# One core, attention and a top-1 mixture of experts: new planner numbers, one last store behind all branches

## The chip, the core and the metric

The kernel runs on one core of one Trainium2 chip. The metric is the device time of one execution in microseconds (us). Five engines work side by side, each with its own list of instructions: TensorE (PE, matrix products and transposes), VectorE (DVE), ScalarE (ACT), GpSimd (POOL) and SyncE (SP), which here issues most of the transfers. An engine runs its list in the order in which it was written; an instruction whose input is not there holds up everything behind it on that engine.

## What is computed

The input is q, k, v of shape (4, 8, 576, 64) and a small memory per head. Attention comes first, and its rows are the tokens of the second part:

```python
scores = scale * np.matmul(q, k.transpose(0, 1, 3, 2))
scores = np.where(causal, -1000000000.0, scores)
scores = scores - scores.max(-1, keepdims=True)
a = np.exp(scores)
a /= a.sum(-1, keepdims=True) + 1e-09
local = np.matmul(a, v)
...
return (g * mem_out + (1 - g) * local).astype(np.float32)
```

Here mem_out is phi(q) times the memory matrix of the head over phi(q) times its norm vector. Then 2304 tokens of 512 numbers are each sent to one of 8 experts:

```python
expert_idx = np.argmax(logits, axis=1)
...
gate_w = probs[np.arange(N), expert_idx]
for e in range(E):
    mask = expert_idx == e
    h = np.maximum(x[mask] @ w1[e], 0.0)
    out[mask] = gate_w[mask, None] * (h @ w2[e])
```

with w1 of 512 x 1024 and w2 of 1024 x 512 per expert.

## The kernel before

**Attention** is cut into 8 groups (a batch, four heads), each with five blocks of query rows, 112 units in all. A unit is worked on by four engines in turn: scores on PE (S, lines 685 and 693), mask and row minimum on DVE (M, line 696), the exponential on ACT (E, lines 724 and 726), transposes of the result on PE (T, lines 733 and 737), copies of the transposed blocks out of the matrix engine's memory on ACT (line 745) or DVE (line 747), and the product with v on PE (C, lines 760 and 768). When the units of a block are done, the assembly adds the memory's share: its matrix product on PE (line 846), a copy on ACT (line 861), small quotients on DVE (lines 867, 887, 897), a product on DVE (Xl, line 907), another on POOL (A, line 913) and their sum on POOL (line 919). The routing then reads the finished rows (line 955 on ACT squares and sums them, lines 969 to 976 cut them in two halves of 16 bits).

**What sets the order.** The class Sched (lines 40 to 185) is a planner. Each operation has an engine, or a list of engines to choose from, a duration, what it depends on, buffers and a priority. The planner simulates the engines and writes the instructions out in the order in which its simulation starts them. The durations of ACT and DVE come from c_act and c_dve (lines 23 and 27), the time after which another engine may use a result from LAT (line 44), that for the same engine from line 109, and the priorities from the table PRIO (line 37), an entry of which ('ra', 'rr', 'aA' and others) can also say which engines an operation may go to. Where the plan leaves PE idle, line 270 puts small filler products. The first steps of the expert part, three tiles of tokens among them, are planned by the same class: the weights come by DMA as 32-bit numbers and are split into a leading part (line 1292 on ACT, 1304 for the second matrix) and a rest (line 1294 on DVE), and the tokens of a tile are gathered by POOL (line 1436).

**The expert loop** is written by hand, one slot of 128 tokens after another: gather the tokens by their row numbers (ix, loaded by SP at line 1421; gather at line 1436 on POOL), transpose and split them, first product (line 1499), relu (line 1508), transposes (line 1512), split (lines 1516 and 1520), second product (line 1526), times the gate value (y_out, line 1532 on DVE, into one of three buffers ys), and a store to the rows of the output that ix names (y_store, an indirect DMA on POOL, line 1550). Slots 0 to 14 (NFIX = 15) always run. Slots 15 to 24 are nested branches: whether a slot has tokens is read from a table (line 1669), and its instructions run only if it has (when, lines 1747 and 1751). With these inputs 19 slots and three tiles ahead of them run, 22 stores in all. The result of slot i-1 is multiplied in slot i's code, and stored in the branch of slot i or, if that is not taken, in its Else arm, the last store of the run.

Of the kernel before, what the change touches and what calls it, by code (L numbers as in the profile page):

```python
# [20 lines left out]


def c_act(n, ptr=False):
    return (284 if ptr else 170) + 0.84 * n


def c_dve(n):
    return 150 + 1.042 * n


def c_pool(n):
# [2 lines left out]

BG = 200.0

PRIO = {'po': {'S': -5.883137309853216, 'M': -5.687372506837317, 'E': 1.1512438895455412, 'T': -2.3534222843976242, 'H': -2.2397011500929547, 'L': -4.132349736948786, 'C': -0.056339306635263986}, 'pa': 1.8585493879096298, 'pv': -5.3741376405058645, 'sq': -21.965205397914144, 'xt': 2, 'ra': 0, 'aD': 1, 'ps': 1.7384297857956093, 'lv': 25.117654926616954, 'pr': 0.9204950267468823, 'rs': 0, 'w1p': 182.12895601615688, 'ag': 0, 'pb': 8.752629265291922, 'lqk': -7.732031619747982, 'rr': 2, 'aA': 1, 'pe4': 2, 'ep': 144.67457595060114, 'w2p': 291.50948210051763, 'slack': 37.2962196981224, 'pp': 1.1250262799121031, 'fc': (1, 2), 'nw2l': 3, 'nw1l': 4, 'xlo': 1, 'wpd': 1, 'w1': 300000, 'ND': 2, 'avl': 2, 'ph': 3, 'avc': 1, 'phat': -15373.102132059515, 'ae': 1, 'rp': 2, 'vhe': 1}


class Sched:  # L40


    TWO = {"xh", "xl", "w1l", "w2l", "exl", "A", "ad", "b", "p", "cu", "est", "eor", "tab", "gn", "gl", "gr"}
    LAT = dict(PE=250, ACT=200, DVE=200, POOL=200, SP=0, NOP=0)

    warm_from, warm_to, warm_ns, warm = 0.0, 0.0, 110, None

# [14 lines left out]
    def run(self, slack=80.0):  # L62
# [15 lines left out]
        while ready:  # L78
            cand = {}
            for o in ready:  # L80
                ts = o["at"]
                ok = True
                for m, al in enumerate(o["alloc"]):
                    ring = al[0]
                    if len(al) > 3:
                        if holder[ring][al[3]] is not None:
                            ok = False
                            break
                        ts = max(ts, self.rings[ring][al[3]])
                        continue  # L90
                    res = (al[2] if len(al) > 2 else 0) + sum(x[0] == ring for x in o["alloc"][:m])
                    fr = sorted(t for t, h in zip(self.rings[ring], holder[ring]) if h is None)
                    if len(fr) <= res:
                        ok = False
                        break
                    ts = max(ts, fr[res])
                if not ok:
                    continue
                best = None
                for eng, dur, fn in o["alts"]:  # L100
                    t = max(ts, free_at.get(eng, 0.0))
                    if eng in port and shares(o, eng):
                        t = max(t, port["DVE" if eng == "POOL" else "POOL"])
                    for d in o["deps"]:
                        p = self.byname[d]
                        if p["xfer"] is not None:
                            lat = 200
                        elif p["eng"] == eng:
                            lat = 0 if eng in ("PE", "SP", "NOP") else (100 if eng == "POOL" else 125 if eng == "DVE" else 120)
                        else:  # L110
                            lat = self.LAT[p["eng"]]
                        t = max(t, p["end"] + lat)
                    if best is None or t + dur < best[1] + best[2]:
                        best = (eng, t, dur, fn)
                cand.setdefault(best[0], []).append((best[1], o["prio"], o["n"], o, best))
# [60 lines left out]
def kernel(  # L176
# [14 lines left out]
    nc = tc.nc  # L191
# [1336 lines left out]
            )  # L1528

    def y_out(i):  # L1530
        ys = big("ys")[(i + NEARLY) % 3]
        nc.vector.tensor_scalar(ys, G[i]["yp"], G[i]["gg"], None, op0=ALU.mult)  # L1532
        G[i]["ys"] = ys

# [9 lines left out]

    out_w = []

    def y_store(i):
        if i < 0:
            nc.gpsimd.memset(pause, 0.0)
        ins = nc.gpsimd.indirect_dma_start(  # L1550
            out=out[:, :], out_offset=bass.IndirectOffsetOnAxis(ap=G[i]["ix"][:, 0:1].bitcast(U32), axis=0),
            in_=G[i]["ys"], in_offset=None, bounds_check=NTOK - 1, oob_is_err=False,
        ).ins

        if i < 0:
            for o in out_w:
                tc.declare_no_dep(ins, o, reason="rows of the output")
            out_w.append(ins)
# [175 lines left out]
    def second(i):  # L1734
        w_dma(2, regs[i]["nx"], cond=regs[i]["pf"])
        if i + 1 < NSLOT:
            gather_g(i + 1)

    def rest(i):

        if i == NSLOT:
            l2(i - 1)
            y_store(i - 1)
            return
        ch_reg(i)
        pf_regs(i)
        with when(i, CALC):  # L1747
            first(i, False)
        l2(i - 1, i)

        with when(i, ALL) as go:
            y_store(i - 1)
            fetch(i + 4)
            second(i)
            rest(i + 1)
        with go.Else():
            y_store(i - 1)

    ch_reg(0)
    pf_regs(0)  # L1760
# [5 lines left out]
    for i in range(NFIX):  # L1766
        first(i)
        l2(i - 1, i)
        y_store(i - 1)
        second(i)  # L1770
    rest(NFIX)


_INS = ["q", "k", "v", "M_prev", "z_prev", "beta", "moe_expert_emb", "moe_tau", "moe_w1", "moe_w2"]
# [26 lines left out]
```

## Time and profile before

| | us |
|---|---|
| median of 3 runs | 542.04 |
| lowest and highest of them | 541.66 and 547.07 |
| the profiled execution, own time | 542.65 |
| its span in the profile | 540.9 |
| PE busy | 515.7 (95%) |
| DVE, ACT, POOL busy | 322.0, 308.8, 185.8 |

The span runs from the first to the last instruction; the own time holds some 1.8 us around it. A share of busy time is an average over parts of the kernel with different limits, so the rows below take it apart by stretches: the attention part up to about 230 us, the passage to the experts up to about 300, the expert loop up to 524, and the end. In a timeline row the bracket says how long the engine had been idle before this instruction and whose result ended the wait.

### The profile page before, as it was taken

To read this page: it belongs to the slowest core of one execution; us is meant where nothing else is said; L and a number is where in the kernel's file an instruction comes from. 1 tells how busy PE (TensorE), PEld (TensorE's weight loads), DVE (VectorE), ACT (ScalarE), POOL (GpSimd) and SP (SyncE) were. 2 spreads that over 40 slices of the span, in tenths; PEclk is the share of its full clock that TensorE was granted. 3 is DMA by queue.
4 is the path that set the end of the run, shared out by engine and by line. 5 is a ranking of instruction groups with operands and counts; after the bars stand their busy time and mean duration, and the time that the engine had idled before them with its cause. 6 is when DMAs were issued, how large, how long until landed. Compare 5 with 4: busy or idle time off the path is not lost. (4 is left out here: it accounts for less than half of the span.)

```text
span 540.9 us, 11357 instructions
## 1 busy us (share of the span) xinstructions
PE 515.7 (95%) x3506; PEld 440.8 (81%) x3506; DVE 322.0 (60%) x1024; ACT 308.8 (57%) x608; POOL 185.8 (34%) x259
## 2 busy tenths in 40 slices
PE   7999999999999999998999999999999999999970
PEld 5888988898898988887877888888888888888850
DVE  5776877777886877777972142522366516863360
ACT  5887877677886877596622252422365526744340
POOL 6101424434443433338445332122331222212221
PEclk9999999999999999999999999999999999999995
DMA  7658745235542311376409846732379846884221
GB/s 156 152 65 186 166 98 118 44 77 133 127 104 46 79 41 41 78 255 154 100 12 243 262 108 217 176 80 59 75 237 320 226 97 213 237 229 152 60 61 34
DMA packets 127471, 71.93 MB, mean 133 GB/s; under 512 B 111385, under 2 KB 111513, under 8 KB 127395
## 3 DMA queue, kind: packets, MB, share of 16 engines
q1 hardware_dynamic: 122242, 59.49, 43.4%
q0 software_dynamic: 5152, 11.57, 7.4%
q8 instruction: 30, 0.49, 0.4%
q14 instruction: 47, 0.38, 0.4%
HBM read 111.74 MB, written 10.67 MB: 226 GB/s over the span
## 5 line engine op out<-in xcount | busy, mean ns | idle before, releaser
L1526 PE MATMUL L<-RC,hhl 128*128 128x512 f32 x528 | 129.0, 394 | 0.3 <-PEq L1747 0.3
L1499 PE MATMUL aux<-RB 128*128 128x512 f32 x528 | 125.8, 392 | 1.6 <-ACTq L1451 1.1
L1499 PEld LDWEIGHTS aux<-RB 128*128 128x128 f32 x528 | 98.3, 188 | 22.6 <-ACTq L1451 1.2
L1526 PEld LDWEIGHTS L<-RC,hhl 128*128 128x128 f32 x528 | 97.5, 188 | 19.9 <-issue 0.7
L1520 DVE TENSOR_TENSOR hhl<-aux,hhl 128x512 fp32r<-128x512 f32 x46 | 31.5, 689 | 118.3 <-ACT hhl L1516 61.4
L760 PE MATMUL L<-VN,aT 128*128 128x128 f32 x640 | 87.3, 276 | 0.0
L760 PEld LDWEIGHTS L<-VN,aT 128*128 128x128 f32 x640 | 79.0, 192 | 2.0 <-DVE aT L747 1.1
L1516 ACT ACTIVATE hhl<-aux 128x512 fp32r<-128x512 f32 x46 | 27.2, 595 | 77.2 <-PE aux L1512 43.1
L696 DVE CUSTOM_DVE_ANT_0 a<-aux,mask 128x128 f32<-128x128 f32 (+3 forms) x144 | 62.2, 451 | 13.7 <-PE aux L685 9.9
L724 ACT ACTIVATE a<-a,nb 128x128 f32<-128x128 f32 (+3 forms) x128 | 65.2, 557 | 0.8 <-DVE nb L696 0.5
L1550 POOL DMA_INDIRECT out_dram<-ys,ix x22 | 22.6, 1026 | 123.5 <-DVE ys L1532 116.3
L733 PE MATMUL aux<-ident,a 128*128 128x128 f32 x384 | 62.4, 280 | 2.6 <-ACT a L724 2.6
L745 ACT ACTIVATE aT<-aux 128x512 f32<-128x512 f32 (+3 forms) x89 | 44.5, 512 | 30.0 <-PE aux L733 29.2
L913 POOL TENSOR_TENSOR A<-ms,dd 128x256 f32<-128x256 f32 x32 | 21.7, 677 | 92.4 <-DVE dd L897 47.9
L733 PEld LDWEIGHTS aux<-ident,a 128*128 128x128 f32 x384 | 43.0, 141 | 12.4 <-ACT a L724 4.4
L1508 ACT ACTIVATE hs<-aux 128x512 f32<-128x512 f32 x44 | 23.9, 595 | 46.6 <-PE aux L1499 46.1
L1436 POOL DMA_INDIRECT a<-x_dram,ix x26 | 28.0, 1075 | 48.3 <-DMA ix<-id_dram 16.5
L1387 DVE TENSOR_TENSOR RB<-RA,RB 128x1024 fp32r<-128x1024 f32 x24 | 29.2, 1225 | 9.1 <-ACT RB L1383 7.8
L1387 DVE TENSOR_TENSOR RC<-RA,RC 128x1024 fp32r<-128x1024 f32 x24 | 27.9, 1221 | 1.7 <-ACT RC L1383 1.5
L1383 ACT ACTIVATE RB<-RA 128x1024 fp32r<-128x1024 f32 x24 | 25.2, 1059 | 6.2 <-PE aux L1499 5.6
L1443 POOL DMA_INDIRECT gg<-gate_dram,ix x23 | 24.6, 1067 | 7.8 <-issue 6.1
L846 PE MATMUL aux<-Mb,qp 128*128 128x130 f32 (+1 forms) x160 | 25.3, 281 | 0.5 <-ACT a L724 0.5
(255 smaller groups left out, 766.1 us busy)
## 6 DMA issues: line engine op xcount, KB each, us to landing
RA<-in_moe_w_dram SPq DMA_DIRECT2D x78, 1024.0 KB
RA<-in_moe_w_dram SPq DMA_DIRECT2D x16, 512.0 KB
RA<-in_k_dram SPq DMA_DIRECT2D x32, 128.0 KB
RA<-in_q_dram SPq DMA_DIRECT2D x32, 128.0 KB
VN<-in_v_dram SPq DMA_DIRECT2D x32, 128.0 KB
x_dram<-x SPq DMA_DIRECT2D x16, 256.0 KB
RA<-in_k_dram SPq DMA_DIRECT2D x8, 64.0 KB
RA<-in_q_dram SPq DMA_DIRECT2D x8, 64.0 KB
```

Source lines behind the costliest of these rows:

```text
L696: nc.vector.tensor_tensor_reduce(out=o, in0=i0, in1=i1, op0=ALU.add, op1=ALU.min, scale=-0.125, scalar=init, accum_out=acc)
L724: nc.scalar.activation(out=a[:, c], in_=a[:, c], func=AF.Exp, scale=-1.0, bias=nb[:, y : y + 1])
L733: nc.tensor.transpose(ps[:, P * y : P * y + P], a[:, P * y : P * y + P], ident)
L745: nc.scalar.activation(out=u["aT"][0:r, o : o + n], in_=t[0:r, 0:n], func=AF.Copy)
L760: nc.tensor.matmul(lt[:, P * hh : P * hh + P], u["aT"][:, P * y : P * y + P], vt[:, c : c + P], start=kb == 0, stop=kb == i)
L846: nc.tensor.matmul(m[rr, 130 * x : 130 * x + 130], qp[:, x, P * i : P * i + n], Mb[b % 2][:, 2 * g + x, :], start=True, stop=True,)
L1387: nc.vector.tensor_tensor(l, s, h.bitcast(F32), op=ALU.subtract)
L1436: nc.gpsimd.indirect_dma_start(out=xg, out_offset=None, in_=x_dram[0:rows, :], in_offset=bass.IndirectOffsetOnAxis(ap=ix[:, 0:1].bitcast(U ...
L1499: nc.tensor.matmul(G[i]["hp"][n], a[:, cc], w[:, c, 512 * n : 512 * n + 512], start=c == 0 and a is xh and w is w1h, stop=c == KD - 1 and ...
L1516: nc.scalar.activation(out=big("hhl")[n][:, 0:512], in_=G[i]["gps", n], func=AF.Copy)
L1520: nc.vector.tensor_tensor(t[:, 512:1024], G[i]["gps", n], t[:, 0:512].bitcast(F32), op=ALU.subtract)
L1526: nc.tensor.matmul(G[i]["yp"], t[:, cc : cc + P], w[:, c, :], start=c == 0 and a == 0 and w is w2h, stop=c == KF - 1 and a == 1)
```

## The change

First, the planner's numbers. The fixed part of an ACT operation falls from 170 (284 with a pointer operand) to 112 (225), that of a DVE operation from 150 to 85; the time until another engine may read the result rises from 200 to 260 and 270, and for the same engine from 120 and 125 to 170 and 180. The priorities are set anew, and with 'aA' the product A may also go to DVE. The matrix products stay the same, but 39 fillers stand where 46 stood, 11 of 32 products A go to DVE, and ten copies of transposed blocks go from DVE to ACT.

Second, the last store. The Else arms with their store go. In each branch taken, and once ahead of the first, POOL copies the row numbers of the slot to a tile of its own (keep, into lix). From slot 14 on all results use one buffer of ys, and one store behind all branches writes that buffer to the rows in lix.

```diff
 def c_act(n, ptr=False):
-    return (284 if ptr else 170) + 0.84 * n
+    return (225 if ptr else 112) + 0.84 * n
...
 def c_dve(n):
-    return 150 + 1.042 * n
+    return 85 + 1.042 * n
...
-    LAT = dict(PE=250, ACT=200, DVE=200, POOL=200, SP=0, NOP=0)
+    LAT = dict(PE=250, ACT=260, DVE=270, POOL=200, SP=0, NOP=0)
...
-                            lat = 0 if eng in ("PE", "SP", "NOP") else (100 if eng == "POOL" else 125 if eng == "DVE" else 120)
+                            lat = 0 if eng in ("PE", "SP", "NOP") else (100 if eng == "POOL" else 180 if eng == "DVE" else 170)
...
     def y_out(i):
-        ys = big("ys")[(i + NEARLY) % 3]
+
+        ys = big("ys")[(i + NEARLY) % 3 if i < NFIX - 1 else 0]
...
-    def y_store(i):
+    def y_store(i, ix=None):
         if i < 0:
             nc.gpsimd.memset(pause, 0.0)
+        ix = G[i]["ix"] if ix is None else ix
         ins = nc.gpsimd.indirect_dma_start(
-            out=out[:, :], out_offset=bass.IndirectOffsetOnAxis(ap=G[i]["ix"][:, 0:1].bitcast(U32), axis=0),
+            out=out[:, :], out_offset=bass.IndirectOffsetOnAxis(ap=ix[:, 0:1].bitcast(U32), axis=0),
...
+    lix = cst.tile([P, 2], I32, name="lix")
+
+    def keep(i):
+        nc.gpsimd.tensor_copy(lix, G[i]["ix"])
+
     def rest(i):
 
         if i == NSLOT:
             l2(i - 1)
-            y_store(i - 1)
             return
...
-        with when(i, ALL) as go:
+        with when(i, ALL):
             y_store(i - 1)
+            keep(i)
             fetch(i + 4)
             second(i)
             rest(i + 1)
-        with go.Else():
-            y_store(i - 1)
...
+    keep(NFIX - 1)
     rest(NFIX)
+    y_store(NFIX - 1, lix)
```

The order of instructions, at three places. The first is PE, group 7 of 8, from a pair of units' scores (128x384, the first two of six rows stand) to the transposes of its first unit, which take the exponentials a_3344 before and a_3341 now. Before:

```order
L685 MATMUL aux_3323<-RB_81 128x384
L685 MATMUL aux_3324<-RB_81 128x384
...
L733 MATMUL aux_3334<-ident_71,a_3248 128x128 x2
L846 MATMUL aux_3341<-Mb0_89,qp1_85 64x130 x2
L768 MATMUL L_3309<-VN2_88,aT_3288 128x130 x5
L733 MATMUL aux_3364<-ident_71,a_3279 128x128 x4
L760 MATMUL L_3373<-VN0_86,aT_3318 128x128 x2
...
L733 MATMUL aux_3400<-ident_71,a_3300 128x128 x4
L846 MATMUL aux_3408<-Mb1_90,qp0_84 128x130 x2
L760 MATMUL L_3373<-VN0_86,aT_3353 128x128 x2
L627 MATMUL aux_3423<-ident_71,RA_80 128x128 x4
L733 MATMUL aux_3431<-ident_71,a_3344 128x128 x3
```

and now:

```order
L685 MATMUL aux_3307<-RB_81 128x384
L685 MATMUL aux_3308<-RB_81 128x384
...
L760 MATMUL L_3128<-VN2_88,aT_3179 128x128 x4
L768 MATMUL L_3335<-VN2_88,aT_3195 128x130 x5
L846 MATMUL aux_3351<-Mb0_89,qp1_85 64x130 x2
L733 MATMUL aux_3357<-ident_71,a_3286 128x128 x4
L733 MATMUL aux_3364<-ident_71,a_3341 128x128 x3
```

Of the work that stood between, eight narrow products of the routing (at the second mark), the scores of another pair, and several blocks have gone elsewhere.

The second place is ACT at the first conversion of weights to the experts' form (L1292, which waits for a DMA). The rows L724 are exponentials, L745 copies, L861 those of the assembly. Before:

```order
L724 ACTIVATE a_3803<-a_3803,nb_3804 128x256 x2
L745 ACTIVATE aT_3858<-aux_3848 128x256
L861 ACTIVATE ms_3879<-aux_3852 64x260
L1292 ACTIVATE RB_81<-RA_80 128x1024
L745 ACTIVATE aT_3941<-aux_3914 128x512
L724 ACTIVATE a_3899<-a_3899,nb_3900 128x384
L745 ACTIVATE aT_3960<-aux_3946 128x512
L861 ACTIVATE ms_3970<-aux_3955 128x260
L724 ACTIVATE a_3928<-a_3928,nb_3929 128x384
```

and now:

```order
L724 ACTIVATE a_3818<-a_3818,nb_3819 128x256 x2
L745 ACTIVATE aT_3924<-aux_3905 128x512
L724 ACTIVATE a_3911<-a_3911,nb_3912 128x384
L1292 ACTIVATE RB_81<-RA_80 128x1024
L724 ACTIVATE a_3927<-a_3927,nb_3928 128x384
L745 ACTIVATE aT_3960<-aux_3930 128x512
L861 ACTIVATE ms_3970<-aux_3954 128x260
L724 ACTIVATE a_3945<-a_3945,nb_3946 128x384
L745 ACTIVATE aT_3992<-aux_3948 128x384
```

One more exponential (a_3911, of 384 columns) stands ahead of the first conversion, and the one of its pair directly behind it.

The third place is the end of POOL's list. Before, each Else arm is like the one whose rows stand here (a semaphore update, shown as ISA, the store, another update, a jump, and then the next arm):

```order
L1796 ISA
L1550 DMA out_0_dram<-ys_4575,ix_3902 2304x512
L1751 ISA
L1751 UNCONDITIONAL_BRANCH
L1796 ISA
```

and now the arms hold an update and a jump, and behind the last of them stand the store and the end:

```order
L1757 ISA
L1757 UNCONDITIONAL_BRANCH
L1552 DMA out_0_dram<-ys_4561,lix_4805 2304x512
L1803 UNCONDITIONAL_BRANCH
L1803 ISA
```

The store has moved from the arm to a place behind the jump, and the arm's update from behind the store to ahead of it.

## Rows read from the trace of the kernel before

**Rows 1.** The page: busy us of each engine, share, instructions

```profile
PE 515.7 (95%) x3506; PEld 440.8 (81%) x3506; DVE 322.0 (60%) x1024; ACT 308.8 (57%) x608; POOL 185.8 (34%) x259
```

**Rows 2.** Stretches: length, busy (instructions) by engine, granted clock, DMA share, GB/s

```profile
0.00:20.00 20.00, 16.10 (x130) 13.01 (x131) 11.26 (x41) 12.43 (x30) 9.28 (x47) 1.00 0.67 145
20.00:220.00 200.00, 199.69 (x1791) 177.74 (x1792) 153.09 (x633) 152.95 (x352) 74.80 (x105) 1.00 0.44 96
220.00:260.00 40.00, 37.58 (x310) 32.70 (x308) 29.80 (x121) 28.74 (x60) 20.50 (x24) 1.00 0.61 168
260.00:300.00 40.00, 38.41 (x217) 31.04 (x217) 24.29 (x106) 14.95 (x27) 20.05 (x25) 1.00 0.53 141
300.00:520.00 220.00, 219.70 (x1046) 183.30 (x1045) 100.03 (x121) 98.55 (x140) 57.13 (x56) 1.00 0.59 167
520.00:541.00 21.00, 4.25 (x22) 3.07 (x21) 3.56 (x6) 1.19 (x2) 4.07 (x4) 0.67 0.12 36
```

**Rows 3.** Waits of PE, 0 to 40: total us, times, longest us

```profile
PE aux L270 <- DVE ident L229: 3.0, 1, 3.0
```

**Rows 4.** Timeline, two rests of PE: start, length, instruction [idle before <-releaser]

```profile
229.92 1.06 ACT L1292 ACTIVATE RB<-RA 128x1024 fp32r<-128x1024 f32 x1 [3.02 <-DMA RA<-in_moe_w_dram]
232.16 0.55 PE L733 MATMUL aux<-ident,a 128*128 128x128 f32 x3 [0.99 <-ACT a L724]
...
243.30 1.68 POOL L913 TENSOR_TENSOR A<-ms,dd 128x256 f32<-128x256 f32 x1
245.82 0.63 ACT L955 ACTIVATE x<-X 128x512 f32<-128x512 f32 x1 [2.89 <-POOL X L919]
247.69 0.66 PE L733 MATMUL aux<-ident,a 128*128 128x128 f32 x4 [1.38 <-ACT a L724]
```

**Rows 5.** Timeline, scores to exponential with nothing in the way

```profile
237.24 0.97 PE L685 MATMUL aux<-RC 64*128 64x512 f32 x6
238.24 0.69 DVE L696 CUSTOM_DVE_ANT_0 a<-aux,mask 128x512 f32<-128x512 f32 x1 [0.32 <-PE aux L685]
239.17 0.71 ACT L724 ACTIVATE a<-a,nb 128x512 f32<-128x512 f32 x1
```

**Rows 6.** The page, a costly group: busy, mean ns | idle before it, releaser

```profile
L1550 POOL DMA_INDIRECT out_dram<-ys,ix x22 | 22.6, 1026 | 123.5 <-DVE ys L1532 116.3
```

**Rows 7.** Timeline of the end

```profile
521.38 2.99 PE L1526 MATMUL L<-RC,hhl 128*128 128x512 f32 x12
521.79 1.02 POOL L1550 DMA_INDIRECT out_dram<-ys,ix  x1 [6.00 <-DVEq L1747]
525.48 0.74 DVE L1532 TENSOR_SCALAR ys<-L,gg 128x512 f32<-128x512 f32 x1
527.19 0.99 POOL L1443 DMA_INDIRECT gg<-gate_dram,ix  x1 [0.31 <-issue]
528.86 1.02 POOL L1550 DMA_INDIRECT out_dram<-ys,ix  x1 [0.67 <-DVEq L1751]
```

**Rows 8.** Four lines: duration ns min/median/max, first and last start us

```profile
L1550 POOL DMA_INDIRECT out_dram<-ys,ix x22: 1005/1026/1067, 296.3 to 528.9; - x22
DMA to landing us min/median/max: 2.7/4.4/7.6
...
L1669 ACTq TENSOR_LOAD <-tab x10: 272/279/822, 471.3 to 524.3; - x10
L1669 POOLq TENSOR_LOAD <-tab x5: 283/293/504, 474.9 to 526.2; - x5
...
L1751 POOLq INC_SWDGE_SEM  x1: 1960/1960/1960, 530.6 to 530.6; - x1
L1751 ACTq EVENT_SEMAPHORE  x2: 17/17/17, 527.8 to 527.9; - x2
...
L1796 POOLq DRAIN  x3: 40/107/7348, 532.8 to 540.7; - x3
L1796 POOLq INC_SWDGE_SEM  x1: 1210/1210/1210, 526.8 to 526.8; - x1
```

More of the change, by code (lines that the diff above doesn't have):

```diff
@@ L35 @@
 BG = 200.0
-PRIO = {'po': {'S': -5.883137309853216, 'M': -5.687372506837317, 'E': 1.1512438895455412, 'T': -2.3534222843976242, 'H': -2.2397011500929547, 'L': -4.132349736948786, 'C': -0.056339306635263986}, 'pa': 1.8585493879096298, 'pv': -5.3741376405058645, 'sq': -21.965205397914144, 'xt': 2, 'ra': 0, 'aD': 1, 'ps': 1.7384297857956093, 'lv': 25.117654926616954, 'pr': 0.9204950267468823, 'rs': 0, 'w1p': 182.12895601615688, 'ag': 0, 'pb': 8.752629265291922, 'lqk': -7.732031619747982, 'rr': 2, 'aA': 1, 'pe4': 2, 'ep': 144.67457595060114, 'w2p': 291.50948210051763, 'slack': 37.2962196981224, 'pp': 1.1250262799121031, 'fc': (1, 2), 'nw2l': 3, 'nw1l': 4, 'xlo': 1, 'wpd': 1, 'w1': 300000, 'ND': 2, 'avl': 2, 'ph': 3, 'avc': 1, 'phat': -15373.102132059515, 'ae': 1, 'rp': 2, 'vhe': 1}
+PRIO = {'po': {'S': -5.883137309853216, 'M': -4.840438712750229, 'E': 1.967546345052414, 'T': -4.114076516220706, 'H': -1.3645901555529374, 'L': 1.3442908904845117, 'C': 1.6431593916058935}, 'pa': 1.8585493879096298, 'pv': -5.20593629974371, 'sq': -20.99193318998207, 'xt': 2, 'ra': 1, 'aD': 1, 'ps': 2.2552552086851994, 'lv': 30.532415533677106, 'pr': -0.844234866969447, 'rs': 0, 'w1p': 132.04025303536926, 'ag': 0, 'pb': 9.02547963519804, 'lqk': -7.242174695271864, 'rr': 0, 'aA': 2, 'pe4': 2, 'ep': 136.46772209101903, 'w2p': 333.3626569704931, 'slack': 37.867454952859006, 'pp': 1.1250262799121031, 'fc': (1, 2), 'nw2l': 3, 'nw1l': 4, 'xlo': 1, 'wpd': 1, 'w1': 300000, 'ND': 2, 'avl': 2, 'ph': 3, 'avc': 1, 'phat': -12849.512758097562, 'ae': 1, 'rp': 2, 'vhe': 3, 'vle': 3, 'oc': 2}
 class Sched:
     TWO = {"xh", "xl", "w1l", "w2l", "exl", "A", "ad", "b", "p", "cu", "est", "eor", "tab", "gn", "gl", "gr"}
-    LAT = dict(PE=250, ACT=200, DVE=200, POOL=200, SP=0, NOP=0)
+    LAT = dict(PE=250, ACT=260, DVE=270, POOL=200, SP=0, NOP=0)
     warm_from, warm_to, warm_ns, warm = 0.0, 0.0, 110, None
```

## The prediction

> **What bounds the kernel now.** I read the page's first lines, then the busy time by stretches, then the timeline of the places where the matrix engine rests, then the end of the span. TensorE is busy 515.7 us, 95% of the span [rows 1]; the others stand at 34 to 60%. By stretches [rows 2] it rests 3.90 us in 0 to 20 (16.10 busy of 20.00), 0.31 in 20 to 220, 2.42 in 220 to 260, 1.59 in 260 to 300, 0.30 in 300 to 520 and 16.75 in 520 to 541. The granted clock is 1.00 in each but the last (0.67, mostly after the work has ended). So the attention part is a nearly full matrix engine with short rests, the expert loop is full, and the only large rest is the end: the last matrix products start at 521.38 and take 2.99 us [rows 7], and 540.9 - 524.4 = 16.5 us after them the span ends. 3.0 us of the first rest wait for the identity matrix [rows 3], which the change leaves alone.
>
> **The expert loop (300 to 520): nothing.** The matrix products are the same, and at 219.70 of 220.00 us busy TensorE waits for nobody. Added is one small copy on GpSimd in each open branch; GpSimd sat idle 123.5 us before its 22 stores, 116.3 of them for VectorE's result [rows 6], so the copy lies in that. With one result buffer in place of three, the result of a slot can be written only when the store before it has landed, 2.7 to 7.6 us after its start; the 22 stores start from 296.3 to 528.9, 11.1 us apart in the mean [rows 8], so the buffer is free in time. The close case is the last pair: a store starts at 521.79, and the next result is written at 525.48 [rows 7]. At the median landing (4.4) VectorE then waits 0.7 us, at the longest 3.9; both end before the new place of the last store (below), so they cost nothing.
>
> **The attention part (0 to 300): -0.5 us.** The change moves instructions and takes no matrix product away except a few fillers that stand where TensorE would rest anyhow. 11 sums of the assembly go from GpSimd to VectorE and ten copies of transposed blocks from VectorE to ScalarE; ten copies of at most 0.71 us [rows 5] are 7 us, and ScalarE is free for 300 - (12.43 + 152.95 + 28.74 + 14.95) = 91 us [rows 2]. So busy shares do not decide. What decides is whether the two engines deliver in time, at three kinds of places:
>
> - At 229.92 ScalarE had waited 3.02 us for weights, and because the exponential was queued behind their conversion TensorE rested 0.99 us [rows 4]. In the new order one exponential stands ahead of that conversion and the next one behind it. The weights come when they come; the wait then falls on that next one. Between a gain of 1.0 and nothing; I take nothing, since its transposes follow the first ones' after two small products.
> - At 245.82 ScalarE had waited 2.89 us for GpSimd's assembly, whose sum took 1.68 us, and TensorE rested 1.38 us at 247.69 [rows 4]. In the new order one of two such sums is VectorE's, but GpSimd's gathers now stand ahead of both assemblies. Between 1.4 and nothing; I take -0.5, a third of it.
> - Everywhere else a unit's scores must be masked and exponentiated before its transposes. Where nothing was in the way that took from 238.21 to 239.88, 1.7 us: mask 0.69, exponential 0.71 and the handing over [rows 5]. The new order puts less matrix work between. For the pair of units shown with the change it was 33 products of full size and 8 narrow ones, and now it is 15; at 0.66 / 4 = 0.165 us each [rows 4] that is 5.4 us and now 2.5. An estimate of this kind for all 112 units gives a mean of 6.6 us before and 4.8 now, and a smallest of 2.3 and 1.8. None is under 1.7, but in the thin ones only 0.8 us is left for another instruction in the queue. The cost lies between nothing and the 6.0 us of the second rival; I take nothing, since 0.31 us of rest in 200 says that these engines were far ahead.
>
> The bounds of this part are a gain of 8.22 - 3.02 = 5.2 us, all the rests that the stretches show before 300 without the first, and a loss of 6.0.
>
> **The end: +1.4 us.** Before, the last store starts at 528.86, 0.67 us of it spent waiting for VectorE's branch [rows 7], in the closing arm of the slot that was not taken. Only then GpSimd waits for the gate values (gathered at 527.19), runs a semaphore update of 1.96 us from 530.6, and starts a DRAIN of 7.35 us at 532.8 [rows 7, 8]. Now the arm holds only the wait, the update and a jump, and the store comes behind: 530.6 + 1.96 = 532.6, then 0.2 for the jump (the step from there to the DRAIN at 532.8), 0.3 to issue (as the gather at 527.19 had it), 1.02 for the store: done at 534.1, and the DRAIN at 534.2 instead of 532.8, +1.4. That takes the DRAIN as a piece of constant length. The ends: -5.8 if it shrinks to the 0.107 us that is its median [rows 8] (7.35 - 0.11 saved, 1.4 added), and +5.4 if the end keeps its distance to the store's end (534.1 against 529.9, +4.2) and an update of the kind of 1.21 us [rows 8] is needed as well. I take the constant piece, the nearest to what the rows show: the one long DRAIN starts right behind the work of this queue, which the change only orders anew.
>
> **Sum.** The profiled run's own time is 542.65, of it 540.9 span: -0.5 + 1.4 gives 543.55. The median of the runs lies 0.61 below that run, so I forecast 542.9.
>
> **Rivals.** A measurement here can tell about 1% from no change: below 536.6 is faster, above 547.5 slower.
>
> 1. **The order fills the rests.** All 5.2 us go: 542.9 - (5.2 - 0.5) = 538.2, and 536.8 if the end does not grow either. For it: the rests lie where queues of ScalarE and GpSimd stood in an unlucky order [rows 4]. Below 536.6 only if rests go that the stretches do not show; the ends of matrix products are modelled, so 199.69 busy us of 200 may hide short ones. Against: the weights' wait and the gathers remain.
> 2. **Cover too thin (slower).** In 20 to 220 the transposes wait for exponentials, because a unit that finds one more mask and one more exponential ahead of it takes 1.7 + 0.69 + 0.71 = 3.1 us, more than the 2.5 of the thin places. It decides from the point where half of the stretch is so placed. Price: where queues were crowded, 220 to 260, TensorE rested 2.42 in 40 us, 6% [rows 2]; over 100 us that is 6.0, 548.9, and over all 200 it is 555. Against: VectorE and ScalarE are busy 153 of 200 us each, so the queues have room.
> 3. **GpSimd's jump is dear.** ScalarE read a slot's flag at 524.3 and ran its first instruction behind the branch at 527.8, 3.5 us; GpSimd went from 526.2 to 526.8, 0.6 [rows 8]. If its jump to the store behind all branches costs what ScalarE's did, the store is 2.9 us later: 545.8. For it: no jump of GpSimd in the trace has that target. Against: its own quick one. [...]
> 4. **The DRAIN shrinks.** If it is short, the end still has to see the store land, 2.7 us after its start at 533.1 at the least [rows 8]: 535.8, and 0.8 more to the span's end, as there was behind the DRAIN (540.1). That is 536.6 of span instead of 540.9, and with -0.5 a median of 542.0 - 4.3 - 0.5 = 537.2. For it: it is long once and short twice. Against: nothing in the change takes work from this queue.
>
> That the change does nothing that a clock can see leaves 542, inside the forecast.
>
> **How the numbers follow.** Forecast, 540.5 to 545: 0.47. First rival, 534 to 540.5: 0.20, half of it below 536.6. Second, 545 to 555: 0.14, most of it above 547.5. Third, 544 to 547.5: 0.12. Fourth, 536 to 540: 0.07. Faster 0.10 + 0.01 = 0.11; slower 0.11 + 0.01 = 0.12; the same 0.77. A range that leaves out about one in ten on either side is 537.0 to 547.8; the likeliest case, the first rival's nearer half, the third and the fourth lie in it.
>
> **What would show it.** Right: the rest of TensorE in 20 to 220 stays under 1 us and in the expert loop near zero; the last store starts at 532 to 534; the DRAIN follows it at once and keeps 7.35 us, so that 17.9 us lie between the last matrix product and the span's end instead of 16.5; the rest near 232 stays and the one near 248 shrinks. Wrong: transposes waiting for exponentials in many units (second rival), a gap of 3 us between GpSimd's update and the store (third), a DRAIN of another length (fourth), or an expert loop that starts over 2 us earlier (first). What would overturn the whole sum is another granted clock; the trace before has 1.00 up to 520.

## The result and the profile after

The changed kernel takes 547.52 us in the median, the kernel before 542.73 (20 runs of each, taken together). The ratio is 1.0091 with a 95% interval of 1.0071 to 1.0111: slower by 0.9%, 3.9 to 6.0 us. The profiled execution after has an own time of 547.71 us and a span of 545.9, 5.0 more than the 540.9 of before.

Where the 5.0 us lie is read from two points of the trace: the end of the last matrix product and the end of the span. The stretches after, with the columns of [rows 2]:

```profile
0.00:20.00 20.00, 16.36 (x141) 13.86 (x142) 11.95 (x42) 13.19 (x34) 9.15 (x47) 1.00 0.63 136
20.00:220.00 200.00, 198.10 (x1752) 174.04 (x1752) 150.49 (x625) 152.09 (x352) 68.25 (x94) 1.00 0.45 97
220.00:260.00 40.00, 39.89 (x332) 35.38 (x333) 32.80 (x132) 32.96 (x66) 18.78 (x24) 1.00 0.63 177
260.00:300.00 40.00, 36.97 (x209) 29.79 (x208) 25.49 (x105) 12.43 (x24) 19.87 (x25) 1.00 0.46 121
300.00:520.00 220.00, 219.70 (x1045) 183.10 (x1045) 98.70 (x120) 98.99 (x142) 58.63 (x60) 1.00 0.59 168
520.00:546.00 26.00, 5.59 (x28) 4.19 (x26) 4.90 (x7) 1.45 (x3) 4.28 (x5) 0.68 0.15 39
```

Three things differ from [rows 2]. From 220 to 260 TensorE rests 0.11 us where it rested 2.42: the stalls of [rows 4] have gone. From 20 to 220 it rests 1.90 instead of 0.31, and from 260 to 300 3.03 instead of 1.59. The waits of TensorE in 220 to 300 (us in total, times, longest) name what is late there now:

```profile
PE aux L1499 <- DVE RB L1492: 1.5, 1, 1.5
PE aux L1075 <- DVE roh L1067: 1.5, 1, 1.5
```

Neither stood in the trace of before: roh are the one-hot rows of the routing, and RB of line 1492 the tokens of slot 0. And the end of the program, the timeline first:

```profile
522.73 2.99 PE L1526 MATMUL L<-RC,hhl 128*128 128x512 f32 x12
528.21 1.05 POOL L1436 DMA_INDIRECT a<-x_dram,ix  x1 [3.85 <-issue]
529.56 1.00 POOL L1443 DMA_INDIRECT gg<-gate_dram,ix  x1 [0.31 <-issue]
536.71 1.02 POOL L1552 DMA_INDIRECT out_dram<-ys,lix  x1 [6.15 <-issue]
```

and the sequencer's rows of GpSimd at three lines, as in [rows 8]:

```profile
L1757 POOLq COMPARE_BRANCH  x6: 34/36/50, 476.9 to 535.1; - x6
L1757 POOLq INC_SWDGE_SEM  x1: 1940/1940/1940, 533.1 to 533.1; - x1
...
L1552 POOLq MOVE  x22: 29/29/38, 296.0 to 535.5; - x22
L1552 POOL DMA_INDIRECT out_dram<-ys,lix x1: 1017/1017/1017, 536.7 to 536.7; - x1
...
L1803 POOLq DRAIN  x3: 40/113/8603, 536.5 to 545.7; - x3
```

The last product ends at 522.73 + 2.99 = 525.7, 1.3 later than before (524.4, [rows 7]). From there the span takes 20.2 us more, before 16.5. So 1.3 of the 5.0 us lie ahead of the end of the last product, where the order acts, and 3.7 behind it. Of these, 1.2 lie ahead of the semaphore update (7.4 us after the last product, before 6.2) and 2.5 between the update's start and the span's end (545.9 - 533.1 = 12.8, before 540.9 - 530.6 = 10.3).

### The profile page after: what moved, and what is told of

The parts are those of the page before. It is cut to its first block, busy times and chain, and to the rows that moved or that the text cites. A ratio compares the mean times of both kernels' runs of the same rounds, so it can differ in the third digit from the quotient of the medians.

```text
span 545.9 us, 11359 instructions
## 1 busy us (share of the span) xinstructions
PE 516.6 (95%) x3499; PEld 440.4 (81%) x3499; DVE 324.3 (59%) x1028; ACT 311.1 (57%) x615; POOL 179.0 (33%) x253
## 4 chain that ended last, share of the span: by engine, by line
PE 79%; DMA 7%; ACT 4%; DVE 3%; SPq 2%; issue 2%; POOL 1%; POOLq 0%; ACTq 0%; DVEq 0%
PE L L1526 19%; PE aux L1499 19%; PE L L760 11%; PE aux L733 8%; PE aux L685 6%; DMA a<-x_dram,ix 6%; PE L L768 4%; PE aux L846 3%; PE aux L1512 3%; PE aux L693 2%; PE aux L627 2%; SPq L494 1%; DVE RC L1306 1%; ACT RA L642 1%; ACT a L724 1%
## 5 line engine op out<-in xcount | busy, mean ns | idle before, releaser
L724 ACT ACTIVATE a<-a,nb 128x128 f32<-128x128 f32 (+3 forms) x128 | 65.5, 557 | 3.8 <-DVE nb L696 3.4
L745 ACT ACTIVATE aT<-aux 128x512 f32<-128x512 f32 (+3 forms) x99 | 48.8, 506 | 25.0 <-PE L L760 13.6
L733 PE MATMUL aux<-ident,a 128*128 128x128 f32 x384 | 60.3, 279 | 0.9 <-ACT a L726 0.3
L913 POOL TENSOR_TENSOR A<-ms,dd 128x256 f32<-128x256 f32 x21 | 13.6, 647 | 68.4 <-DVE dd L897 39.1
L919 POOL TENSOR_TENSOR X<-A,Xl 128x256 f32<-128x256 f32 x32 | 23.7, 740 | 23.4 <-DVE A L913 9.4
```

The source lines that it names most:

```text
L724: nc.scalar.activation(out=a[:, c], in_=a[:, c], func=AF.Exp, scale=-1.0, bias=nb[:, y : y + 1])
L733: nc.tensor.transpose(ps[:, P * y : P * y + P], a[:, P * y : P * y + P], ident)
L745: nc.scalar.activation(out=u["aT"][0:r, o : o + n], in_=t[0:r, 0:n], func=AF.Copy)
```

## The experiments

Each ratio is to the kernel before, run on the same chip, with its 95% interval. There are three chips: that of the first four rows, where the kernel before takes 543.9 us in the median; that of plan_w2l, plan_w2d, no_last_store and late_gather, where it takes 548.3; and that of arms_lix, gates_late, after_late and w2d_late, where it takes 546.1. Times and traces of different chips can therefore differ by some us that no edit made. One such place is TensorE's longest wait near 292, for the first slot: in kernels with the old order it is 1.1 us in before and tail_only, and 2.9 to 3.3 in arms_lix, gates_late and late_gather.

| run | what it is | ratio | interval |
|---|---|---|---|
| tail_only | old planner numbers, new last store | 1.0056 | 1.0030 to 1.0081 |
| plan_only | new planner numbers, old Else arms | 1.0029 | 1.0005 to 1.0052 |
| cost_only | new durations, old priorities, Else arms | 1.0163 | 1.0123 to 1.0204 |
| prio_only | old durations, new priorities, Else arms | 1.0239 | 1.0208 to 1.0271 |
| plan_w2l | plan_only, one weights' rest behind the routing | 1.0024 | 0.9987 to 1.0062 |
| plan_w2d | plan_only, all weights' rests on VectorE | 1.0007 | 0.9972 to 1.0042 |
| no_last_store | changed kernel without its last store | 1.0032 | 0.9995 to 1.0069 |
| arms_lix | copies and one buffer, store in the arms | 1.0042 | 1.0011 to 1.0072 |
| late_gather | before, nothing gathered for slots that do not run | 0.9903 | 0.9869 to 0.9938 |
| gates_late | before, only the gate values so | 1.0020 | 0.9992 to 1.0048 |
| after_late | changed kernel with late_gather's gathers | 0.9961 | 0.9934 to 0.9988 |
| w2d_late | plan_w2d with late_gather's gathers | 0.9919 | 0.9883 to 0.9955 |

### The two halves of the change

tail_only takes the change without its planner numbers, plan_only these alone:

```diff
 # tail_only: the kernel before, and
-        ys = big("ys")[(i + NEARLY) % 3]
+        ys = big("ys")[(i + NEARLY) % 3 if i < NFIX - 1 else 0]
...
+            keep(i)
...
-        with go.Else():
-            y_store(i - 1)
...
+    y_store(NFIX - 1, lix)
 # plan_only: the kernel before, and
-    return 150 + 1.042 * n
+    return 85 + 1.042 * n
...
-    LAT = dict(PE=250, ACT=200, DVE=200, POOL=200, SP=0, NOP=0)
+    LAT = dict(PE=250, ACT=260, DVE=270, POOL=200, SP=0, NOP=0)
...
```

> The planner's numbers as before, the last store once behind all branches. Theory A (two separate costs, the end the larger): the update of 1.9 us, the jump and the issue now lie ahead of the store, and the DRAIN of 7.4 us counts from the store's end. From the start of the update to the end of the span 12.8 us instead of 10.3, so +2.5 us at the least and +3.6 if SP's last load of row numbers is later too: 545.2 to 546.3, ratio 1.0046 to 1.0066. Rival B (the new order of the attention part and the passage costs all): the time before, within 0.7 us.

> The new planner numbers, the Else arms with their store as before. Theory A: the 1.3 us by which the last matrix product is later in the trace after remain, the end takes 16.5 us from there as before: about 544.0, ratio 1.0025. In the trace PE waits 1.4 to 1.5 us for VectorE's one-hot rows of the routing (roh) near 267, and the rests between 220 and 260 are nearly gone. Rival B: about 547, all of the difference.

Measured: +0.56% and +0.29%, together 0.85%, about as much as the whole change. Both halves cost, and both results are those of theory A; by the medians the end is the larger, though the two intervals overlap. In tail_only (its last product, its last store, its update, its DRAIN)

```profile
523.21 2.99 PE L1526 MATMUL L<-RC,hhl 128*128 128x512 f32 x12
536.62 1.02 POOL L1552 DMA_INDIRECT out_dram<-ys,lix  x1 [5.98 <-issue]
...
L1757 POOLq INC_SWDGE_SEM  x1: 1948/1948/1948, 533.3 to 533.3; - x1
...
L1803 POOLq DRAIN  x3: 40/113/8605, 536.4 to 545.6; - x3
```

the update starts at 533.3 and the span ends at 545.8, 12.5 us as in the changed kernel, not the 10.3 of before. In plan_only the rests are nearly those of the changed kernel, 1.39 (there 1.90), 0.11 and 3.03 us in three stretches:

```profile
20.00:220.00 200.00, 198.61 (x1760) 174.60 (x1758) 150.60 (x626) 152.19 (x353) 68.28 (x94) 1.00 0.46 97
220.00:260.00 40.00, 39.89 (x333) 35.34 (x330) 32.99 (x132) 32.97 (x65) 18.33 (x23) 1.00 0.64 178
260.00:300.00 40.00, 36.97 (x209) 29.78 (x208) 25.25 (x105) 12.55 (x24) 19.43 (x24) 1.00 0.44 111
```

### Durations without priorities, and the reverse

```diff
 # cost_only: the kernel before, and c_act, c_dve, LAT and line 109 of the change
 # prio_only: the kernel before, and the line PRIO of the change
```

> The new durations and latencies with the old table of priorities, Else arms as before. If the durations as traced make a better plan of themselves, the last matrix product is earlier than 524.4, by up to the 2.4 us that PE rests in 220 to 260 before: 540 to 542.7. If any plan with less matrix work between scores and transposes is worse (the thin cover), PE rests over 1 us in 20 to 220 as in the trace after and the time is 543.5 to 546.

> The old durations with the new table of priorities, Else arms as before. If the table is what puts the routing's rows late (PE waits for roh near 267), that wait of 1.5 us is here too and the time is 543.5 to 545. If the wait comes only from durations and table together, it is absent and the time lies within 1 us of before.

Measured: 1.6% and 2.4% slower, both far outside what was expected. Neither half of the planner's numbers gains alone, and each alone is several times dearer than both together. The waits of TensorE in 255 to 300 name the same stall, first in cost_only:

```profile
PE L L1526 <- DVE RC L1306: 4.1, 1, 4.1
```

and in prio_only:

```profile
PE L L1526 <- DVE RC L1306: 4.2, 1, 4.2
```

VectorE's rest of the second weights comes 4.1 to 4.2 us too late for the second product. The priorities of those operations (w1p, w2p, ep in the table) are numbers that fit one set of durations: under the other, the planner puts the weights' rests behind other work. The wait is not all that this place costs. Behind it the granted clock falls: to 0.58 and 0.57 in 280 to 284 and 284 to 288 of cost_only (0.91 in the mean of 260 to 300, where before and plan_only have 1.00), and 17 products take 6.20 us, where 24 take 5.60 from 292.66 on at 1.00. That is some 2.2 us more, an estimate from these two rows. In prio_only the clock is 0.50 and 0.66 in 292 to 296 and 296 to 300 (0.91 in the mean of 260 to 300 too), and 11 products take 5.06 us, some 2.5 more. The one place thus makes up 6.3 of the 9.9 us by which cost_only's last product is later than before's, but only 6.7 of the 14.5 of prio_only; the rest of prio_only's loss lies at other places (in 20 to 220, for one, TensorE rests 2.63 us).

### What holds up the passage to the experts

In the trace before, VectorE computes three rests of the second weights (L1306), GpSimd starts the fourth (L1307) while the third of them is under way, and the routing's logits are copied by VectorE (L1026) at 264.85. Timeline of before:

```profile
260.66 3.49 DVE L1306 TENSOR_TENSOR RC<-RA,RC 128x1024 fp32r<-128x1024 f32 x3
263.63 2.76 POOL L1307 TENSOR_TENSOR RC<-RA,RC 128x1024 fp32r<-128x1024 f32 x1 [5.33 <-ACT RC L1304]
264.85 0.17 DVE L1026 COPY lrt<-aux 128x8 f32<-128x8 f32 x1 [0.51 <-PE aux L1020]
```

and after, with the end of the logits' product (L1020) and the product that waits for the one-hot rows (L1075):

```profile
260.44 5.69 DVE L1306 TENSOR_TENSOR RC<-RA,RC 128x1024 fp32r<-128x1024 f32 x3
260.85 3.07 POOL L1307 TENSOR_TENSOR RC<-RA,RC 128x1024 fp32r<-128x1024 f32 x1 [3.75 <-ACT RC L1304]
263.49 0.24 PE L1020 MATMUL aux<-enT,xT 128*128 128x8 f16 x4
266.06 0.15 DVE L1026 COPY lrt<-aux 128x8 f32<-128x8 f32 x1
267.60 0.19 PE L1075 MATMUL aux<-roh,tri 128*128 128x24 f16 x1 [1.47 <-DVE roh L1067]
```

The new order starts GpSimd's instruction 2.8 us earlier, beside VectorE's three. These take 5.69 us instead of 3.49. The logits, ready at 263.7, stand behind them in VectorE's list until 266.06, and TensorE waits 1.47 us. Two experiments touch this place:

```diff
 # plan_w2l: plan_only, and
-           deps=(("w2h", c),), prio=cfg.get("w2p", 220.0) + c)
+           deps=(("w2h", c),) + ((("rk", 3),) if c == 2 else ()), prio=cfg.get("w2p", 220.0) + c)
 # plan_w2d: plan_only, and in PRIO
-'nw2l': 3
+'nw2l': 4
```

> The new planner numbers with Else arms, and one more dependence: VectorE's third rest of the second weights (L1306) has to wait for the rank products of the fourth routing batch. Theory A (three such instructions stand ahead of the routing logits and two of them run beside GpSimd's one, 5.7 us instead of 3.5): with two ahead the logits are read 1.5 to 2 us earlier, PE's wait of 1.5 us for roh near 267 goes, and the loop starts 0.9 to 1.3 us earlier: ratio to before 0.998 to 1.001 where plan_only had 1.003. Rival (the wait moves to the next link, the tokens of slot 0 near 292, or to the second product that wants these weights): 1.002 to 1.004, and in the trace PE waits as long in 260 to 300.

> The new planner numbers with Else arms, and all four rests of the second weights on VectorE, none on GpSimd. Theory A (VectorE and GpSimd hold each other up when both run them): the four take 4 x 1.2 = 4.9 us in place of 5.7 for three, the logits are read 0.5 to 1 us earlier, ratio 0.999 to 1.002. Rival (the number of instructions ahead of the logits counts, not the sharing): the logits are read no earlier, 1.003 or more.

With nothing on GpSimd beside them, plan_w2d's three take the old time, and the logits are copied right behind:

```profile
261.31 3.50 DVE L1306 TENSOR_TENSOR RC<-RA,RC 128x1024 fp32r<-128x1024 f32 x3
264.73 0.16 DVE L1026 COPY lrt<-aux 128x8 f32<-128x8 f32 x1
```

In plan_w2l GpSimd's instruction stays where it is, and two of VectorE's still take

```profile
263.90 4.55 DVE L1306 TENSOR_TENSOR RC<-RA,RC 128x1024 fp32r<-128x1024 f32 x2
```

So the sharing is shown: 3.5 us for three without GpSimd's instruction, 4.55 for two with it. The rows of the changed kernel one by one tell how: VectorE's first takes 1.23 us from 260.44, its second 3.42 from 261.58, its third 1.21 from 264.9, and GpSimd's runs from 260.85 to 263.92. So 2.25 us of GpSimd's row lie behind the end of VectorE's first (261.67), and 1.1 us of VectorE's second behind the end of GpSimd's: the two seem to take turns, and the lengthening of 2.2 us is then GpSimd's turn. The trace before agrees: GpSimd's row, started at 263.63 beside VectorE's third, ends 2.24 us behind that one's end (264.15), and VectorE's three keep 1.21 to 1.22 us each. That they take turns is an estimate from these rows; what the two engines share is not shown. The wait for roh is gone in both runs, yet both times agree with plan_only's within the intervals. (1.0007 of plan_w2d is also what its theory A had; the run can't tell it from 1.0029.) In plan_w2d's waits of 255 to 300 stands the next link:

```profile
PE aux L1485 <- DMA a<-x_dram,ix: 1.7, 1, 1.7
PE aux L1499 <- ACTq L1451: 1.1, 1, 1.1
```

TensorE now waits for the tokens of slot 0, gathered after the routing. In plan_w2l it waits 1.3 us for them, 1.6 for ScalarE's branch of line 1451, and 1.4 for the rest that was put back. The passage is a chain (last attention rows, routing, row numbers, gather, first slot), and an earlier link moves the wait to a later one: the rival expectation of plan_w2l. The cleanest pair for this is after_late and w2d_late (below), on one chip and both without the needless gathers: the one has the waits of the changed kernel for roh and RB, the other those of plan_w2d, and the last product starts at 523.92 and 523.91. That the stalls of 220 to 260 went gained nothing fits this chain; how much each link took was not measured.

### What the end consists of

```diff
 # no_last_store: the changed kernel, and
-    y_store(NFIX - 1, lix)
 # arms_lix: tail_only, and
+        with go.Else():
+            y_store(NFIX - 1, lix)
...
-    y_store(NFIX - 1, lix)
```

> The changed kernel without its last store (the last 128 rows of the output are left out); copies of the row numbers and the one buffer stay. Theory A (the DRAIN's 7.4 us count from the end of GpSimd's last work, which is the store): the DRAIN's end falls from 7.4 us behind the store to 7.4 us behind the update and its jump. In the trace after the update ends at 535.0, the store at 537.7, the span at 545.9: the span's end comes 2.2 to 2.7 us earlier, ratio to before 1.004 to 1.005 instead of 1.009. Rival (the length comes from the update or from the gathers that nobody uses): no change, the store was hidden in the DRAIN.

> The kernel before with the copies of the row numbers and the one buffer, but the last store in the Else arms, from the copied row numbers. Theory A (the place of the store behind the update and the jump is the cost, not the copies or the buffer): the time of before, ratio 0.998 to 1.002, and from the start of the update to the end of the span 10.3 to 10.7 us. Rival (the copies, or VectorE waiting for the one buffer, cost): 1.003 or more, with VectorE's last scaling late.

no_last_store gives 1.0032, with an interval from no difference to 1.0069, which leaves out the 1.009 of its rival; the trace says more than the time. Its last product, its update and its DRAIN:

```profile
526.96 3.02 PE L1526 MATMUL L<-RC,hhl 128*128 128x512 f32 x12
...
L1757 POOLq INC_SWDGE_SEM  x1: 1940/1940/1940, 540.2 to 540.2; - x1
...
L1802 POOLq DRAIN  x3: 40/107/7331, 542.7 to 550.6; - x3
```

From the update's start to the span's end (550.8) 10.6 us instead of 12.8: the store behind the update is worth 2.2 us, as theory A has it, and the DRAIN is 7.33 us again. In the changed kernel the DRAIN's row shows 8.60, but it starts at 536.5, before the store; behind the store's end, 536.71 + 1.02 = 537.7, it lasts to 545.1, 7.4 us. The DRAIN is a piece of nearly constant length behind GpSimd's last work. That this run's last product is as late as 530.0 comes in part from ahead: TensorE waits 3.2 us for slot 0's tokens, and the granted clock is 0.57 in the 4 us behind that wait (0.96 in the mean of 260 to 300).

arms_lix, whose store stands in the arms again, was expected to take the time of before. It takes 0.42% more (0.11 to 0.72), which the rival expectation had. Its trace:

```profile
524.33 2.99 PE L1526 MATMUL L<-RC,hhl 128*128 128x512 f32 x12
532.79 1.05 POOL L1436 DMA_INDIRECT a<-x_dram,ix  x1 [6.83 <-issue]
536.17 1.02 POOL L1552 DMA_INDIRECT out_dram<-ys,lix  x1 [1.02 <-POOLq L1758]
...
L1758 POOLq INC_SWDGE_SEM  x1: 1960/1960/1960, 537.4 to 537.4; - x1
...
L1805 POOLq DRAIN  x3: 40/107/7350, 539.6 to 547.5; - x3
```

From the update's start to the span's end (547.8) it is 10.4 us, so the place of the store does decide that piece. But the update starts 10.1 us behind the last product (524.33 + 2.99 = 527.3), before 6.2, because the gather at 532.79 is late. gates_late (below), which has neither the copies nor the one buffer, has 8.1 on the same chip, and the kernels with Else arms and three buffers 6.7 to 7.8. The other kernel with copies and one buffer on a slower chip, no_last_store, has 10.2 too. On the chip of tail_only there is no such difference: 7.1 with copies and one buffer, 6.7 to 7.3 without. In arms_lix and no_last_store the last load of row numbers takes 3.1 and 4.0 us to the gather, in the others with that gather 2.5 to 2.9, and VectorE waits 0.46 us for the one buffer in arms_lix. Whether the copies and the buffer cost some of the delay, or the transfers were slow in these two runs, stays open: the kernel before has no trace on these two chips. So the time of arms_lix does not part it from tail_only (their intervals overlap), and that the place of the store costs is shown by the piece behind the update and by no_last_store.

### What the update waits for

In the kernel before the update starts 3.4 us after the issue of the last gather, and the last two gathers serve slots that do not run. The idea is that the update waits for every gather under way. late_gather moves them behind the question whether the slot runs; gates_late does so for the gate values alone; after_late and w2d_late put late_gather's lines into the changed kernel and into plan_w2d.

```diff
 # late_gather: the kernel before, and (second takes a flag that leaves out its gather_g)
             y_store(i - 1)
-            fetch(i + 4)
-            second(i)
+            gather_g(i)
+            if i + 4 < NSLOT:
+                with when(i + 4, (ET.SP, ET.Pool)):
+                    fetch(i + 4)
+            second(i, False)
...
-        second(i)
+        second(i, i < NFIX - 1)
 # gates_late: the same with
+            gather_g(i)
+            fetch(i + 4)
+            second(i, False)
```

> The kernel before, in which a branched slot fetches the gate values only when it runs itself and the tokens of slot i+4 only if that slot has any, so that nothing is gathered for slots that do not run. Theory A: at the end GpSimd waits for no gather (before: until 530.5 for the gate values of a slot that was not taken), the update starts right behind the last store (529.9) or beside it, the DRAIN 0.8 to 2.0 us earlier: 0.997, 541 against 542.7. Rival (the update takes its 1.96 us wherever it stands and the extra branches delay SP and GpSimd in the loop): no gain, or slower by up to 1 us.

> The kernel before, where a branched slot fetches its own gate values; the tokens of slot i+4 are fetched as before. Theory A (the update waits for whatever gather is still under way, and the tokens' gather, issued 1.3 us ahead of the gate values, lands 0.6 us ahead of them): most of the gain of late_gather stays away, ratio 0.997 to 1.000. Rival (the gate values' gather alone is what the update waits for): 0.990 to 0.994, as late_gather.

> The changed kernel with the gathers of late_gather. Theory A (the store behind the update costs 2.2 to 2.6 us whatever the update waits for): the gain of late_gather, 1.0%, is taken from the 0.9% of the changed kernel, ratio to before 0.998 to 1.001. Rival (the store behind the branches is dear only because the update waits for gathers): 0.993 to 0.995, late_gather plus the 0.3% of the planner's numbers.

> The new planner numbers with all four rests of the second weights on VectorE, Else arms, and the gathers of late_gather. If both add up, ratio 0.9903 + 0.0007 = 0.991; it beats late_gather only if the rests of 220 to 260 that the new order saves are not lost again at slot 0's tokens near 292, which the trace of plan_w2d makes unlikely.

late_gather is 0.97% faster than before (0.6 to 1.3), 5.2 us by the medians, over twice the 2.0 us that were the most expected. Its end:

```profile
525.45 3.00 PE L1526 MATMUL L<-RC,hhl 128*128 128x512 f32 x12
527.16 1.04 POOL L1443 DMA_INDIRECT gg<-gate_dram,ix  x1 [0.30 <-issue]
531.48 1.01 POOL L1550 DMA_INDIRECT out_dram<-ys,ix  x1 [3.28 <-POOLq L1751]
...
L1751 POOLq INC_SWDGE_SEM  x1: 1847/1847/1847, 531.6 to 531.6; - x1
...
L1799 POOLq DRAIN  x3: 40/107/6940, 533.7 to 541.2; - x3
```

The update starts 3.2 us behind the last product (528.45), right beside the last store, where it was 6.2 to 10.2 in the kernels that gather for absent slots. The span ends at 541.4, 13.0 us behind the product instead of 16.5. My expectation counted from the trace of before alone; in the other runs of Else arms with three buffers and these gathers the end took 17.1 to 18.5, so it is a stretch that varies between runs; in the two runs with Else arms and without these gathers (late_gather and w2d_late) it took 13.0 and 13.1. gates_late (1.0020; its theory A had 0.997 to 1.000) shows that the tokens' gather alone is enough to hold the update up: with the tokens still fetched nothing is gained, and the update at 536.8 comes 4.0 us after their gather at 532.75. Whether the gate values alone would be enough was not tried. The tokens' chain is long: SP loads the row numbers (523.39 before, 525.75 after), GpSimd gathers 2.5 us later, and the update of gates_late comes 4 us behind that.

after_late is 0.39% faster than before, between its two expectations, and behind late_gather (0.9903) and w2d_late (0.9919). Its end, and two lines of w2d_late from the same chip:

```profile
523.92 2.99 PE L1526 MATMUL L<-RC,hhl 128*128 128x512 f32 x12
532.81 1.02 POOL L1552 DMA_INDIRECT out_dram<-ys,lix  x1 [6.06 <-DVEq L1757]
...
L1757 POOLq INC_SWDGE_SEM  x1: 1830/1830/1830, 528.7 to 528.7; - x1
...
L1806 POOLq DRAIN  x3: 40/113/8193, 532.6 to 541.4; - x3
```

```profile
523.91 3.01 PE L1526 MATMUL L<-RC,hhl 128*128 128x512 f32 x12
...
L1751 POOLq INC_SWDGE_SEM  x1: 1847/1847/1847, 530.1 to 530.1; - x1
```

In after_late the update starts 1.8 us behind the last product, and from it to the span's end (541.6) are 12.9 us. In w2d_late, whose last product ends at the same time, the update starts at 530.1 and the span ends 9.9 us later, at 540.0. So behind the update's start the new place costs 3.0 us also where no needless gather is waited for, as theory A has it. But 1.4 us of them come back: the update no longer stands behind a store that waits for VectorE, and starts earlier. The net cost is 1.6 us in these two traces. The wait for VectorE falls on the new store instead: it starts at 532.81, 2.3 us after the update's end, when VectorE, done with the scaling at 529.3, has come to the end of its branch at 532.2. w2d_late, at 0.9919, is level with late_gather: the planner's new numbers add nothing to it. Both beat the kernel before.

## Why the prediction was right or wrong

The forecast was 542.9 us with a range of 537.0 to 547.8, and no difference beyond 1% as the likeliest. The measured 547.5, and the ratio of 1.0091, lie inside, near the slow edge; of the difference of 4.8 us the forecast had 0.9. That it lies inside is owed to the width of the range and not to the sum: the time is outside the 540.5 to 545 that the forecast itself was given, at the edge of the third rival's stretch and within the second's, and neither of these two came true. Of the signs that were to show it right, the DRAIN's length held and the expert loop rested no more than before, while the rest in 20 to 220, the start of the last store (536.7, not 532 to 534), the 17.9 us of the end (20.2) and the rest near 232 (gone) did not.

- **The expert loop, nothing: right.** TensorE is busy 219.70 of 220 us in 300 to 520, before and after, and the results come at the same distance.
- **The attention part, -0.5 us: wrong in sign.** plan_only measures +0.29%, 1.6 us (0.3 to 2.8); its last product is 1.0 us later than before's, that of the changed kernel 1.3. The two stalls that were priced went further than taken: 2.3 us of rest between 220 and 260 (first rival). (What the text calls sums of the assembly there, 11 of them and the one of 1.68 us, are the products A of line 913; the prices do not hang on it.) The step that failed is the list of three kinds of places: it had none for the passage of 260 to 300, where the change also moved instructions. GpSimd's rest of the weights came beside VectorE's, ahead of the routing, the wait went there, and the rest of that passage grew from 1.59 to 3.03 us. The bound of the loss, 6.0, held.
- **Cover too thin (second rival): nearly nothing.** The rest in 20 to 220 grew from 0.31 to 1.90, over the 1 us that I had set as the mark. Of what the waits name there, 0.9 is a wait for q from memory, and waits for exponentials are 0.5 us in two instances. The mark was passed, by another cause in the larger part.
- **The end, +1.4 us: right mechanism, mis-sized.** tail_only measures 3.0 us (1.6 to 4.4); its trace has 3.1, that of the changed kernel 3.7. The DRAIN is the nearly constant piece that I took. Two terms of the sum were short. From the update's end to the store I had 0.2 + 0.3 us; it took 536.71 - (533.1 + 1.94) = 1.7, because the store behind the branches waits for semaphores once more and is issued 0.8 us after the last of them. And I took the update's start as given at 530.6, though it came 6.2 to 7.8 us behind the last product in kernels of the same arms, and moves when the gathers are left out. The copies and the one buffer, which I put at nothing, are not shown to be free: arms_lix has both and takes 0.42% more, of which their part stays open.
- **GpSimd's jump (third rival): no.** The branch of 535.1 is followed by the first instruction behind it at 535.5, 0.4 us. On TensorE's queue the longest branch of the same line lasts 3727 ns, on GpSimd's 50; why the two queues differ is not shown.
- **A shorter DRAIN (fourth rival): no.** It is 7.3 to 7.4 us behind the last work in the eight runs named below that gather for absent slots, 6.9 to 7.0 in the three that do not.

## What to carry to other kernels

Of the 20.2 us behind the changed kernel's last product 12.8, from the update on, are one chain on GpSimd's queue. For such an end, list what the last engine waits for ahead of its last store, and ask of each whether anybody needs it; here leaving out the gathers for slots that never run gained 0.97%, as much as the whole change lost. An update or a wait placed ahead of a store lies in front of the store with its whole length, even if the arm looks shorter: here the update's 1.94 us and 1.7 us more. A planner's durations and its priorities are one setting: change them together, and look at the next link of the chain before a stall that vanishes is counted as a gain.

## What was not expected of the hardware

GpSimd's DRAIN lasts 7.3 to 7.4 us behind its last indirect transfer or update in eight runs with unneeded gathers (before, after, tail_only, plan_only, plan_w2d, no_last_store, arms_lix, gates_late), and 6.9 to 7.0 in the three without (late_gather, after_late, w2d_late); the timelines show no work of another engine in that time. What it waits for is not shown; it is as long without the last store (7.33 us in no_last_store).

The first products take 1.6 to 1.7 times as long as the same ones later (in the trace before four transposes of line 597 take 1.09 us at 5.02 and 0.66 at 9.29), and for how long differs between executions: in the trace before twelve products of 64x128 at 8.06 took 0.90 us, in tail_only, with the same order up to there,

```profile
8.06 1.54 PE L685 MATMUL aux<-RB 64*128 64x128 f32 x12
```

while the granted clock stands at 1.00 in both. In the first 20 us tail_only gets through 112 products, before 130. Its logits' product is 1.7 us later at 266, and its last product 1.8 us later than before's, so this start explains nearly all of it: a part of the spread between runs that has nothing to do with the change. The traces of the changed kernel and of plan_only show no such slow start (0.96 us for the twelve products).
